# Half of each v load moved from the SP queue to GpSimd's own DMA queue

## The chip, the cores and the metric

The kernel runs on one core of a Trainium2 chip. The metric is the device time of one execution in microseconds (us), the median over the runs of a kernel. Lower is better.

## The reference

Two attentions in a row, then a mixture of experts with one expert per token. Cut to what is computed:

```python
# q, k, v: [8, 8, 576, 64], p: [8, 8, 32, 64], scale = 1/8
p_packed = softmax(scale * p @ k^T) @ v            # 32 packed rows per head
out      = softmax(scale * q @ p_packed^T) @ p_packed
x = out.transpose(0, 2, 1, 3).reshape(4608, 512)
logits = x @ w_gate + modality_bias[modality_id]    # 8 experts
e = argmax(logits); g = softmax(logits)[e]
y = g * (relu(x @ w1[e]) @ w2[e])                   # w1: 512 x 1024, w2: 1024 x 512
```

All inputs and the output are float32.

## The kernel before, in words

**Attention units.** A unit is one pair of batches (i = 0 to 3) and one group of four heads (g = 0, 1), so there are eight units, m = 0 to 7. A unit loads its k, q and v, each 1152 KB, each as two DMAs of 576 KB (u = 0, 1: the two batches of the pair). `load_tok` (L192 to L197) loads k and q: each of its two DMAs writes rows of 2304 bytes to all 128 partitions. `load_v` (L204 to L209) loads v: the DMA of u = 0 writes partitions 0 to 63, the one of u = 1 writes partitions 64 to 127. All of them are issued by SP (SyncE), whose DMAs go through one queue in order, as do the stores of the attention's result to scratch memory (`xout`, L379 and L380) and the loads of the experts' weights (`load_w`, L644).

**What a unit computes.** `trans` (L215) turns k and q on TensorE, `scores1` (L229, L239 to L246) makes the first softmax, `a1trans` (L260) turns it, and `pack` (L266 to L287, matmuls at L273) multiplies it with v. For each of nine column blocks, `pack` takes the half of u = 0 and the half of u = 1 in turn, so it wants both halves nearly from its first matmul. VectorE (DVE) then scales the result at L281 (tile `bd`), and `packT`, `gate`, `scores2`, `xpart` and `xout` (L289 to L383) make the second attention and store it. v's tile comes from a pool of even units or a pool of odd units with one buffer each, so the v load of unit m waits for `pack` of unit m - 2.

**Order.** The loop at L779 walks n from -6 to 11 and, for each n, a list of steps written by hand (`ORDER`, L401). A step's leading > or < says which unit it is for: `>>>>dk`, `>>>dq` and `>>dv` issue the loads of k, q and v for units n + 4, n + 3 and n + 2. So SP's order at the start is k0, packed rows p, k1, q0, v0, k2, q1, then the constants of `routing_consts` (L98: two stores of a padding list at L100, a bias load at L104, two loads of modality numbers at L108), then v1, k3, q2, v2 and so on. The program order of PE, DVE, ACT and SP is fixed by this list (`manual_schedule`, L778); that of GpSimd (POOL) is not among them, and a planner places its instructions. In the loop GpSimd has the casts and products of `routing_consts` (L119 to L128), which wait for the load at L108, and the scattered writes of `scatter` (L469, nine for each pair of batches). After the loop it fetches token rows (L660, L662).

**After the loop.** Units 0 to 6 go through the loop, the rest of unit 7 is woven into the first expert slots. From about 150 us on the expert matmuls (L695, L730) run one slot after the other.

Of the kernel before, what the change touches and what calls it, by code (L numbers as in the profile page):

```python
# [17 lines left out]
DRAM = bass.MemoryType.DRAM  # L18
ds = bass.ds
SYNC = mybir.DependencyInfo(mybir.DependencyClass.Sync, mybir.DependencyReason.DATA)  # L20


@with_exitstack
def packed_attn_moe_kernel(
# [14 lines left out]
    nc = tc.nc  # L39
# [9 lines left out]
    SP = S // NC  # L49
# [82 lines left out]
    NA = (NP // 2, NP - 1)  # L132
# [34 lines left out]
    def prep_p(ps1, n4):  # L167
# [5 lines left out]
        nc.vector.tensor_copy(out=pT[:, n4:n4 + 4, :], in_=t.rearrange("p (n c) -> p n c", n=4))  # L173
        yield

# [6 lines left out]
    def attention(i, g, lt, A, Z):  # L185
# [3 lines left out]
        hs = slice(HG * g, HG * g + HG)  # L189
        D_ = {}  # L190

        def load_tok(src, nm):  # L192
            t = A["ld"].tile([P, 2, 2, NC * D], F32, name="re" + nm)
            for u in range(2):
                nc.sync.dma_start(t[:, u], src[2 * i + u, hs].rearrange("h s d -> (h s d)").rearrange(
                    "(a r x) -> r a x", r=P, x=NC * D))
            return t  # L197

        def tile_of(nm, pool, shape, **a):
# [3 lines left out]

        def load_v():  # L204
            v_t = zp.tile([P, HG, NC * D], F32, name="ld_v")
            for u in range(2):
                nc.sync.dma_start(v_t[SP * u:SP * u + SP], v[2 * i + u, hs].rearrange("h s d -> h (s d)").rearrange(
                    "h (p x) -> p h x", x=NC * D))
            return v_t.rearrange("p h (c d) -> p h c d", c=NC)  # L209

        def trans(nm, f0, w):
# [173 lines left out]
        def load(nm):  # L385
            D_[nm + "r"] = load_v() if nm == "v" else load_tok(k if nm == "k" else q, nm)
            yield
# [23 lines left out]
    def ins_of(x):  # L411
        return getattr(x, "ins", x)
# [52 lines left out]
    def scatter(i):  # L465
        for c in range(NC):
            dsi = sm.tile([P, 1], I32, name=f"dsi{c}", bufs=2)
            nc.vector.tensor_copy(out=dsi, in_=dests[i][:, c:c + 1])  # L468
            ins = ins_of(nc.gpsimd.indirect_dma_start(  # L469
                out=lst, out_offset=bass.IndirectOffsetOnAxis(ap=dsi, axis=0),  # L470
                in_=meta[:, i * NC + c, :], in_offset=None))
            tc.declare_no_dep(ins, group="scat", reason="every row of the list is written once")
            tc.add_to_no_dep_group("scat", ins)
            if i >= NA[0]:
                tc.add_to_no_dep_group("late", ins)
            if i >= NA[1]:
                tc.add_to_no_dep_group("last", ins)
            scattered[i].append(ins)
            yield ins
# [178 lines left out]
    def fetch(tb, s, ph, mt, xt):  # L658
# [8 lines left out]
        if ph == 1:  # L667
            for z in scattered[NA[1] - 1]:
                tc.add_manual_dep(ins_of(ins[0]), z.name, SYNC, reason="rows of the list")

# [11 lines left out]
    def behind(ins, todo, n_each):  # L682
        for _ in range(n_each):
            z = next(todo, None)
            if z is not None:
                tc.add_manual_dep(z, ins.name, SYNC, reason="scatters with time between them")

# [54 lines left out]
    with ExitStack() as actx:  # L742
# [32 lines left out]
        for n in range(NA[0]):  # L775
            more[2 * n + 2] = route(n)
            spread[2 * n + 2] = scatter(n)
        with tc.manual_schedule(engines={ET.PE, ET.DVE, ET.Activation, ET.SP}):  # L778
            for n in range(-6, NU + 6):  # L779
                for z in ORDER.split():  # L780
                    nm = z.lstrip("<>")
# [33 lines left out]
    first = (0, SA[0], SA[1])  # L815
# [79 lines left out]
    with ExitStack() as actx:  # L895
# [4 lines left out]
        u = us[NU + 1]  # L900

        def table_b():
            for _ in routing(NA[1] - 1, lts[NA[1] - 1], ZL["ps1"]):
                pass
            T.append(table_phase("b", T[0]["last"], NA[1], T[0]["used"], SA[1] - SA[0]))
            todo.append(scatter(NA[1] - 1))
# [13 lines left out]
        with behind_both(first_x):  # L920
            split_w(W, 0, None, (1, 2, 3))
            for _ in routing(NA[1] - 1, lts[NA[1] - 1], ZL["ps1"]):
                pass
        todo.append(scatter(NA[1] - 1))
        for n in range(1, 4):
            ev = st_1(W, todo[0], 3, (2 * n,))
# [71 lines left out]
```

## Time and profile before

| what | us |
|---|---|
| median of 3 runs | 621.76 |
| lowest and highest run | 619.72, 625.98 |
| the profiled execution | 618.04 |
| its span, first to last instruction | 616.4 |
| around the span | 1.64 |
| TensorE busy in the span | 573.3 |
| VectorE busy | 252.3 |
| ScalarE busy | 219.9 |
| GpSimd busy | 148.1 |

PE is TensorE's matmuls and PEld its weight loads; DVE is VectorE, ACT ScalarE, POOL GpSimd, SP SyncE. An engine's busy time is an average over stages with different limits: in the attention stage the DMA engines are full, in the expert stage TensorE is. Times in the rows are counted from the start of the span. v0 is the v load of unit 0, and likewise k3 or q1; the first half of a v load is u = 0, the second u = 1.

### The profile page before, as it was taken

The numbers are of one execution on the slowest core, as the hardware profiler recorded it, in microseconds if no ns is written. First come the engines' busy times: TensorE is split into PE (matmuls) and PEld (weight loads), VectorE is DVE, ScalarE is ACT, GpSimd is POOL, SyncE is SP. The second block draws the span as 40 slices with busy tenths as digits, with TensorE's granted clock in tenths as the row PEclk, the third lists the DMA queues.
The fourth block names the chain that finished last, engine by engine and source line by source line (L and its number), as shares of the span: only waits on it lengthen the run. The fifth ranks groups of instructions, "written<-read, shape, count | busy, mean of one in ns | idle before, by whom it ended". The sixth has DMA issues, their size and how long they took to land. (4 is left out here: it accounts for less than half of the span.)

```text
span 616.4 us, 12544 instructions
## 1 busy us (share of the span) xinstructions
PE 573.3 (93%) x4820; PEld 499.8 (81%) x4820; DVE 252.3 (41%) x669; ACT 219.9 (36%) x401; POOL 148.1 (24%) x183
## 2 busy tenths in 40 slices
PE   4879898987999999999999999999999999999982
PEld 3657676665988989889889889989989989989981
DVE  1468998985965412145021173112112112112281
ACT  3648676755433111153121272122122112112360
POOL 2020041350552332232123122212211211311221
PEclk9979999976999999999999999999999999999997
DMA  9999999968766410028603027111201111111111
GB/s 292 248 262 314 313 347 308 299 144 299 250 225 174 155 53 20 36 85 341 275 25 99 36 74 287 64 43 37 66 38 36 51 39 52 48 40 53 41 49 56
DMA packets 49224, 87.47 MB, mean 142 GB/s; under 512 B 12528, under 2 KB 22320, under 8 KB 49136
## 3 DMA queue, kind: packets, MB, share of 16 engines
q1 hardware_dynamic: 39024, 63.92, 32.5%
q0 software_dynamic: 8528, 22.16, 11.3%
q8 instruction: 48, 0.79, 0.5%
q10 hardware_dynamic: 1584, 0.28, 0.2%
q14 instruction: 40, 0.33, 0.2%
HBM read 66.78 MB, written 19.56 MB: 140 GB/s over the span
## 5 line engine op out<-in xcount | busy, mean ns | idle before, releaser
L695 PE MATMUL ps_h<-x_hl,w1h 128*128 128x256 f32 x1088 | 199.6, 285 | 0.8 <-ACTq L892 0.7
L695 PEld LDWEIGHTS ps_h<-x_hl,w1h 128*128 128x128 f32 x1088 | 171.8, 193 | 4.5 <-ACT x_hl L677 1.0
L695 PE MATMUL ps_h<-x_hl,w1l 128*128 128x256 f32 x544 | 154.4, 284 | 0.0
L700 DVE SCALAR_TENSOR_TENSOR hl<-ps_h,hh 128x512 fp32r<-128x512 f32 x68 | 46.9, 690 | 245.8 <-ACT hh L699 245.7
L730 PE MATMUL ps_o<-w2h,hh 128*128 128x512 f32 x296 | 118.1, 399 | 3.0 <-ACT ot L734 2.2
L730 PE MATMUL ps_o<-w2h,hl 128*128 128x512 f32 x296 | 116.4, 393 | 0.0
L730 PE MATMUL ps_o<-w2l,hh 128*128 128x512 f32 x296 | 115.8, 391 | 0.3 <-DVEq L845 0.3
L695 PEld LDWEIGHTS ps_h<-x_hl,w1l 128*128 128x128 f32 x544 | 104.8, 193 | 0.0
L699 ACT ACTIVATE hh<-ps_h 128x512 fp32r<-128x512 f32 x68 | 40.6, 597 | 151.2 <-PE ps_h L695 149.7
L735 POOL DMA_INDIRECT out_dram<-ot,mt x37 | 40.7, 1100 | 183.6 <-ACT ot L734 119.1
L734 ACT ACTIVATE ot<-ps_o,mt 128x512 f32<-128x512 f32 x37 | 25.4, 688 | 149.6 <-PE ps_o L730 123.2
L730 PEld LDWEIGHTS ps_o<-w2h,hh 128*128 128x128 f32 x296 | 55.7, 188 | 14.7 <-ACT ot L734 3.5
L469 POOL DMA_INDIRECT lst<-meta,dsi x36 | 36.6, 1017 | 119.3 <-DVE dsi L468 63.2
L730 PEld LDWEIGHTS ps_o<-w2h,hl 128*128 128x128 f32 x296 | 55.6, 188 | 11.6
L730 PEld LDWEIGHTS ps_o<-w2l,hh 128*128 128x128 f32 x296 | 55.7, 188 | 10.9 <-DVEq L845 0.6
L662 POOL DMA_INDIRECT xt<-x_scr,mt x46 | 45.3, 984 | 74.1 <-DMA mt<-lst 28.2
L218 ACT COPY kT<-ps 128x512 f32<-128x512 f32 (+1 forms) x80 | 40.9, 555 | 24.5 <-PE ps L215 24.5
L678 DVE TENSOR_TENSOR x_hl<-ps_t,x_hl 128x512 fp32r<-128x512 f32 x42 | 27.5, 683 | 19.5 <-ACTq L845 12.0
L215 PE MATMUL ps<-ident,rek 128*128 128x128 f32 x144 | 23.2, 302 | 7.8 <-DMA rek<-in_k_dram 7.5
L660 POOL DMA_DIRECT2D mt<-lst x23 | 17.3, 753 | 54.0 <-DMA out_dram<-ot,mt 40.1
L354 PE MATMUL ps<-bd,a2T 64*128 64x136 f32 (+1 forms) x320 | 27.0, 320 | 3.1 <-DVE a2T L338 2.4
L273 PE MATMUL ps<-ld_v,a1T 64*64 64x128 f32 x576 | 21.8, 291 | 7.4 <-DMA ld_v<-in_v_dram 5.9
(187 smaller groups left out, 642.7 us busy)
## 6 DMA issues: line engine op xcount, KB each, us to landing
raw<-in_moe_w_dram SPq DMA_DIRECT2D x24, 1024.0 KB
rek<-in_k_dram SPq DMA_DIRECT2D x16, 576.0 KB
req<-in_q_dram SPq DMA_DIRECT2D x16, 576.0 KB
ld_v<-in_v_dram SPq DMA_DIRECT2D x16, 576.0 KB
x_scr<-xs SPq DMA_DIRECT2D x28, 256.0 KB
x_scr<-ld_v SPq DMA_DIRECT2D x4, 256.0 KB
x_scr<-xs SPq DMA_DIRECT2D x14, 64.0 KB
raw<-in_p_dram SPq DMA_DIRECT2D x2, 384.0 KB
```

What stands on the lines that cost most here:

```text
L215: nc.tensor.transpose(out=t[:, c * P:c * P + P], in_=src[:, (f0 + c) * P:(f0 + c) * P + P], identity=ident)
L218: nc.scalar.copy(out=T_[:, f0:f0 + w, :], in_=t[:, :w * P].rearrange("p (f r) -> p f r", f=w))
L354: nc.tensor.matmul(xp[rows, pr, z * XW:z * XW + XW], a2T[rs, t0:t0 + n], D_["bd"][rs, u, :], start=True, stop=True)
L469: ins = ins_of(nc.gpsimd.indirect_dma_start(out=lst, out_offset=bass.IndirectOffsetOnAxis(ap=dsi, axis=0), in_=meta[:, i * NC + c, :], in_ ...
L662: ins.append(nc.gpsimd.indirect_dma_start(out=xt[:, t], out_offset=None, in_=x_scr[0:NA[ph] * 2 * S] if ph < 2 else x_scr, in_offset=bass. ...
L678: iv = tt(out=M["xl"][:, :, ts], in0=ps, in1=M["xh"][:, :, ts].bitcast(F32), op=ALU.subtract)
L695: nc.tensor.matmul(ps[:, f], M[a][:, j, (f0 + f) * P:(f0 + f) * P + P], M[b][:, j], start=(n == 0), stop=(n == 3 * KD - 1))
L699: ia = nc.scalar.activation(out=M["hh"][:, fs], in_=ps, func=AF.Relu)
L700: iv = nc.vector.scalar_tensor_tensor(out=M["hl"][:, fs], in0=ps, scalar=0.0, in1=M["hh"][:, fs].bitcast(F32), op0=ALU.max, op1=ALU.subtract)
L730: nc.tensor.matmul(op, M[a][:, j, t * P:t * P + P], M[b][:, j, :], start=(n == 0), stop=(n == 3 * KF - 1))
L734: nc.scalar.activation(out=ot, in_=op, func=AF.Copy, scale=mt.bitcast(F32)[:, t, 2:3])
L735: nc.gpsimd.indirect_dma_start(out=out, out_offset=bass.IndirectOffsetOnAxis(ap=mt[:, t, 1:2], axis=0), in_=ot, in_offset=None, bounds_che ...
```

## The change

Of the two DMAs of a v load, the one of u = 1 (partitions 64 to 127) is now issued by GpSimd, on GpSimd's queue, and the one of u = 0 stays on SP. The GpSimd issues of v halves and the scattered writes of pairs 0 and 1 are chained in program order (`on_pool`), without a wait between them. For the two units of pair 0 (v0 and v1) the GpSimd issue also waits until the second half of that unit's q load has landed (`landed`). The chain does not name the casts of `routing_consts`.

```diff
+NOSYNC = mybir.DependencyInfo(mybir.DependencyClass.NoSync, mybir.DependencyReason.DATA)
...
+    landed = []
+    in_order = []
+
+    def on_pool(ins):
+        if in_order:
+            tc.add_manual_dep(ins, in_order[-1].name, NOSYNC, reason="the loop's order")
+        in_order.append(ins)
...
             for u in range(2):
-                nc.sync.dma_start(t[:, u], src[2 * i + u, hs].rearrange("h s d -> (h s d)").rearrange(
+                ins = nc.sync.dma_start(t[:, u], src[2 * i + u, hs].rearrange("h s d -> (h s d)").rearrange(
                     "(a r x) -> r a x", r=P, x=NC * D))
+            if nm == "q":
+                landed.append(ins_of(ins))
...
         def load_v():
             v_t = zp.tile([P, HG, NC * D], F32, name="ld_v")
-            for u in range(2):
-                nc.sync.dma_start(v_t[SP * u:SP * u + SP], v[2 * i + u, hs].rearrange("h s d -> h (s d)").rearrange(
+            for u, q_ in ((1, nc.gpsimd), (0, nc.sync)):
+                ins = q_.dma_start(v_t[SP * u:SP * u + SP], v[2 * i + u, hs].rearrange("h s d -> h (s d)").rearrange(
                     "h (p x) -> p h x", x=NC * D))
+                if u == 1:
+                    on_pool(ins_of(ins))
+                    if i == 0:
+                        tc.add_manual_dep(ins_of(ins), landed[g].name, SYNC, reason="k and q first")
...
+            if i < NA[0]:
+                on_pool(ins)
```

## Rows read from the trace of the kernel before

**Rows 1.** Windows by stage: length, busy us of each engine (instructions), PEclk, DMA share, GB/s.

```profile
36.00:44.00 8.00, 5.22 (x88) 4.12 (x88) 3.14 (x9) 1.76 (x4) 0.34 (x1) 0.59 1.05 331
...
60.00:128.00 68.00, 59.67 (x1002) 44.78 (x1002) 63.30 (x233) 46.78 (x100) 16.17 (x17) 0.96 1.04 310
...
152.00:582.00 430.00, 425.94 (x2799) 385.96 (x2799) 126.60 (x304) 110.90 (x183) 108.83 (x111) 1.00 0.29 98
```

**Rows 2.** Windows of the attention stage by which load is moving, same columns.

```profile
16.00:21.00 5.00, 4.84 (x47) 3.43 (x47) 1.32 (x5) 4.19 (x10) 0.00 (x0) 1.00 1.05 218
...
22.00:27.00 5.00, 4.83 (x99) 3.43 (x100) 2.49 (x6) 1.37 (x4) 0.00 (x0) 1.00 1.05 393
28.00:32.00 4.00, 4.00 (x64) 2.95 (x70) 2.58 (x6) 3.25 (x8) 0.18 (x2) 1.00 0.27 32
...
34.00:38.00 4.00, 1.43 (x10) 0.97 (x10) 3.93 (x9) 3.69 (x8) 2.27 (x3) 0.94 1.05 222
...
125.00:128.00 3.00, 2.36 (x50) 1.16 (x50) 2.90 (x12) 1.67 (x4) 0.86 (x2) 0.71 1.05 223
```

**Rows 3.** PE timeline, pack's matmuls of units 0, 1, 3 and 5.

```profile
22.17 0.88 PE L273 MATMUL ps<-ld_v,a1T 64*64 64x128 f32 x22 [1.21 <-DMA ld_v<-in_v_dram]
...
24.97 0.89 PE L273 MATMUL ps<-ld_v,a1T 64*64 64x128 f32 x24
...
36.51 0.40 PE L273 MATMUL ps<-ld_v,a1T 64*64 64x128 f32 x2 [1.48 <-DVE nb L242]
39.18 4.11 PE L273 MATMUL ps<-ld_v,a1T 64*64 64x128 f32 x70 [2.28 <-DMA ld_v<-in_v_dram]
...
68.91 2.20 PE L273 MATMUL ps<-ld_v,a1T 64*64 64x128 f32 x72
...
103.93 2.19 PE L273 MATMUL ps<-ld_v,a1T 64*64 64x128 f32 x70 [2.40 <-DMA ld_v<-in_v_dram]
```

**Rows 4.** Waits of DVE, 20 to 60 us: total us, times, longest.

```profile
DVE bd L281 <- PE ps L273: 5.5, 3, 4.8
```

**Rows 5.** Waits of DVE, 60 to 130 us, all of them.

```profile
DVE lt L367 <- ACT xs L365: 1.7, 4, 0.6
DVE r L252 <- ACT a L246: 1.0, 2, 0.8
DVE bd L281 <- PE ps L273: 0.5, 1, 0.5
```

**Rows 6.** SP timeline, DMA issues around the first v loads.

```profile
11.70 1.37 SPq L207 DMA_DIRECT2D ld_v<-in_v_dram  x2
...
15.45 10.05 SPq L100 DMA_DIRECT2D lst<-pad  x2
25.54 3.56 SPq L104 DMA_DIRECT2D bias<-n_moe_modality_bias_dram  x1
29.15 1.50 SPq L108 DMA_DIRECT2D mid<-in_moe_modality_id_dram  x2
30.69 1.29 SPq L207 DMA_DIRECT2D ld_v<-in_v_dram  x2
```

**Rows 7.** POOL timeline: the casts' first and last, a plain DMA and the gather behind it.

```profile
31.82 0.35 POOL L119 CAST m<-mid 64x16 f32<-64x16 int32 x2 [27.04 <-DMA mid<-in_moe_modality_id_dram]
...
35.55 0.79 POOL L128 TENSOR_TENSOR bias_all<-bias_all,bias_t 128x288 f32<-128x288 f32 x1
...
132.25 0.78 POOL L660 DMA_DIRECT2D mt<-lst  x1 [2.01 <-DMA lst<-meta,dsi]
...
134.62 1.03 POOL L662 DMA_INDIRECT xt<-x_scr,mt  x1 [0.67 <-DMA mt<-lst]
```

**Rows 8.** Windows around two falls of TensorE's clock, columns as in rows 1.

```profile
33.00:37.00 4.00, 1.67 (x12) 1.04 (x10) 3.93 (x9) 3.93 (x8) 3.17 (x7) 1.00 1.00 242
...
39.00:44.00 5.00, 4.82 (x86) 3.94 (x86) 0.61 (x2) 0.00 (x0) 0.00 (x0) 0.50 1.05 392
...
71.00:75.00 4.00, 2.03 (x29) 0.95 (x25) 3.90 (x11) 1.50 (x5) 0.00 (x0) 1.00 1.08 384
75.00:78.00 3.00, 2.91 (x14) 2.91 (x15) 2.72 (x19) 1.50 (x6) 0.00 (x0) 0.51 1.03 257
```

**Rows 9.** DVE timeline: one small operation beside a busy POOL, and alone.

```profile
34.99 0.52 DVE L328 TENSOR_SCALAR dn<-dn 128x18 f32<-128x18 f32 x1
...
45.30 0.17 DVE L328 TENSOR_SCALAR dn<-dn 128x18 f32<-128x18 f32 x1
```

## The prediction

> **What bounds the kernel now.** I read the windows by stage first. From 152 to 582 us TensorE is busy 425.9 of 430 us at full clock, with the DMA engines 29% busy [rows 1]: the expert stage is bound by TensorE and loads no v, so the change can only move its start. In the attention stage, from 60 to 128 us, the DMA engines stand at 1.04 and VectorE (DVE) at 63.3 of 68 us [rows 1]. Two resources look full there, so the waits must say which ends last. DVE waits 3.2 us in all from 60 to 130 us, and only 0.5 of it leads back to pack, the user of v [rows 5]; from 20 to 60 us pack holds it 5.5 us, 4.8 of them in one piece [rows 4]. That piece is the second unit's pack: from 36 to 44 us DVE is busy 3.1 of 8 us [rows 1]. So after 60 us DVE sets the pace and a faster load is mostly absorbed, and around 38 us a load sets it.
>
> Next, the windows by kind of load. While k and q (128 partitions) are loaded the queue moves 393 GB/s; while v is loaded it moves 218, 222 and 223, at an equal DMA share [rows 2], the first, second and last of eight such stretches. A v half is 576 KB = 0.590 MB, so it takes 0.590/217 = 2.72 us and a unit's v 5.4 us, where k takes 3.0. From 28 to 32 us the DMA engines are nearly idle, 0.27 and 32 GB/s [rows 2]: SP had issued v0 from 11.70 us, and is then held for 10.05, 3.56 and 1.50 us by the constants' small DMAs before it issues v1 at 30.69 [rows 6].
>
> Last, the PE timeline: pack waits for v three times, 1.21 us at 22.17 (unit 0), 2.28 us at 39.18 (unit 1) and 2.40 us at 103.93 (unit 5) [rows 3]. Sum 5.9 us. That is all that v costs TensorE directly.
>
> **The change part by part.**
>
> *v1, the main term.* Two matmuls of pack 1 run at 36.51, with the first half, and the other 70 wait until 39.18 [rows 3]: what is late is the second half, behind the first on SP's queue, behind the constants. With the change GpSimd issues it once q1 has landed. The rate falls from 393 GB/s to nothing by 28 us [rows 2], so q1 has landed by about 28.0. For GpSimd's path the nearest row is a plain DMA of 4 KB: begun at 132.25, and the gather that needs it starts at 134.62, so 2.37 us or less from begin to landing [rows 7]. The half then lands at about 28.0 + 2.4 + 2.7 = 33.1 us, largely in the idle stretch, where it takes nothing from anyone. The first half still lands before 36.5, as it does now. So pack 1 runs through from 36.5 and the wait goes: **-2.28 us**. Ends: 0 (the half comes no sooner) and -4.7 (the clock, next). DVE idles 4.8 us there [rows 4], so it can take even the larger gain, and after it no load must wait for the compute: v2's second half may also go out in the idle stretch, as pack 0, whose tile it reuses, ends at 24.97 + 0.89 = 25.9 us [rows 3]. That frees 2 x 2.72 = 5.4 us of SP's queue for k and q, more than the 2.3 us by which the compute moves up.
>
> *The clock at pack 1.* [...] Pack 1's 70 matmuls take 4.11 us there, 72 take 2.20 at full clock [rows 3]. If the clock stayed up, another 4.11 - 2.14 = 2.0 us would go, and some 0.5 on the scores behind. I don't take it: the idle before 36.5 stays, since its last part is a wait for DVE (1.48 us, [rows 3]), and at 71 to 75 us 2.03 busy us in 4 were followed by 0.51 as well [rows 8]. It is a case of its own.
>
> *v0.* q0 has landed near 16 us, where the rate falls to 218 with v0 [rows 2]. GpSimd's half then flows from about 16.0 + 2.0 = 18 us, when the first half is nearly through (16.0 + 2.7 = 18.7), and shares the engines with k2. Now both halves need 16.0 + 5.4 = 21.4 us, and pack's wait ends at 22.17 [rows 3]. With half of 393 GB/s GpSimd's half needs 0.590/196 = 3.0 us, to 21.0; with half of the time at 217 GB/s 5.4 us, to 23.4, which is 2.0 later than 21.4. Taken: 0, nearer to the first. Ends: -1.2 (the whole wait) and +2.0.
>
> *v2 to v7.* Packs 2, 3, 4, 6 and 7 don't wait for v (unit 3's at 68.91 stands for the five in [rows 3]), so a v that comes sooner is worth nothing there by itself. At 103.93 TensorE waits 2.40 us, but DVE works on through it: its whole wait for pack after 60 us is 0.5 us [rows 5]. Taken: -0.5, ends -1.2 and 0.
>
> *What is added.* Eight issues leave SP (1.37 us for a pair, [rows 6]) and eight come to GpSimd, at 0.78 [rows 7] to perhaps 1.5 us each, as the half has as many rows to describe as 256, but longer ones. GpSimd is busy 16.2 of 68 us from 60 to 128 [rows 1], which covers 8 x 1.5 = 12; without that cover the scattered writes would be late, but the list is read only after 130 us. What is queued behind a waiting v half on GpSimd: for v1 the casts of the constants, which wait for their load until 31.82 anyway [rows 7]; for v4 to v7 scattered writes, each held at most until pack of two units earlier, which is long done. A busy GpSimd slows a small DVE operation from 0.17 to 0.52 us [rows 9]; eight issues, one or two such meetings: **+0.3**, ends 0 and 8 x 0.35 = 2.8.
>
> *Whether two queues help each other.* No row shows two half loads at once. The nearest are 218 and 393 GB/s [rows 2], so side by side the halves take between 2.7 and 5.4 us. My sum takes little from this: v1 gains because GpSimd is not held by SP's constants, not because the halves overlap.
>
> [...]
>
> *Sum.* -2.28 + 0 - 0.5 + 0.3 = -2.5 us. The profiled execution of 618.04 (616.4 of span and 1.64 around it) becomes 615.5. It lies 3.7 us below the median of the runs shown, 621.76, and from that the forecast is 621.76 - 2.5 = **619.3 us**. The three runs lie 619.72 to 625.98, 1% apart, so 1% (6.2 us) is about what can be told from no change.
>
> **The rivals.**
>
> *B, the clock stays up.* A pack 1 that runs on at 36.5 keeps TensorE above its low level, and v0 comes 0.8 us sooner. [...] -2.5 - 2.0 - 0.5 - 0.8 = -5.8, so 616.0.
>
> *C, the halves take turns.* Packets of both queues go through the same engines, and a half load beside other traffic gets half the time at 217 GB/s. Then v0 is 2.0 us late (23.4 against 21.4), the compute up to pack 1 moves by as much, and of the 2.28 us 0.3 is left, which DVE's slowing of 0.3 takes: 0.0, so 621.8. For it: the DMA share is already 1.05 at 218 GB/s [rows 2]. [...]
>
> *D, slower: v1's half stands behind the casts on GpSimd.* The chain names v halves and scattered writes, not the casts, and the planner places those. Behind them the half is issued at 35.55 + 0.79 = 36.3 [rows 7], lands at 36.3 + 2.4 + 2.7 = 41.4, or 44.1 beside k3, so pack 1 is 2.2 to 4.9 us later than 39.18, at a point where DVE has nothing else to do [rows 4]. It decides once the issue is later than 39.18 - 5.1 = 34.1 us. +3.5, so 625.3. Against it: q1 lands some 4 us before the casts can start, and a planner that places what is ready first puts the half ahead.
>
> *E, it doesn't do what it says.* GpSimd's half is early, but the first half, still behind SP's constants, comes after 36.5 and pack 1 waits for that one. Two matmuls with it ran at 36.51 [rows 3], so at best a fraction is lost. I count it with C.
>
> **How the numbers follow.** My forecast 0.48, B 0.20, C with E 0.20, D 0.12. The forecast's own range is 616 to 622. To hold 8 in 10 it must reach past B and C, take v0's ends (-1.2, +2.0) and 2.8 us of DVE's slowing, and much of D: 612 to 625. Faster by over 1% needs 615.5 or less: half of B and a tenth of the forecast, with the spread of the runs, 0.22. Slower by over 1% needs 628: half of D, and C with the slowing on top, 0.10. Within 1% is the rest, 0.68.
>
> **What would show it right or wrong.** Right: one large DVE wait for pack before 60 us shrinks from 4.8 to about 2.5; DMA traffic appears between 28 and 33 us; pack 1's matmuls start near 36.5 without a wait for v, still at 0.50; waits of DVE after 60 us stay near 3 us. B: PEclk is 1.00 from 37 to 44. C: unit 0's pack starts after 23 us, and half loads beside each other stay near 217 GB/s. D: GpSimd's issue of v1 stands after L128. The forecast is wrong at its root if DVE's waits after 60 us fall or grow by several us, for then the loads, not DVE, set the pace of the loop; or if the expert stage itself, 430 us that I leave untouched, changes its length.

## The result and the profile after

| what | before, us | after, us |
|---|---|---|
| median (11 runs each) | 621.17 | 625.56 |
| lowest and highest run | 619.64, 625.98 | 623.75, 628.76 |
| the profiled execution | 618.04 | 625.72 |
| its span | 616.4 | 624.0 |
| start of the first expert matmul | 150.90 | 155.50 |
| from there to the end of the span | 465.5 | 468.5 |

The ratio is 1.0064, interval 1.0041 to 1.0088: 4.0 us slower (2.5 to 5.5). That is less than 1%, but the median lies 0.6 us above the range of 612 to 625, and on the other side of before than the forecast of 619.3. The profiled execution of before lies 3.1 us under its median and that of after 0.2 above, so the two profiles differ by 7.6 us of span where the medians differ by 4.4: what follows reads places and shares from the profiles and sizes from the ratios. Of the 7.6 us, 4.6 arise before the expert stage and 3.0 in it.

The PE timeline of after (start and duration in us; in brackets the idle time before and what ended it), matmuls of pack, line 291 now: three rows of unit 0, one each of units 1, 3 and 5, and three of the seven pieces of unit 7:

```profile
27.02 1.55 PE L291 MATMUL ps<-ld_v,a1T 64*64 64x128 f32 x22 [5.95 <-DMA ld_v<-in_v_dram]
...
29.54 1.56 PE L291 MATMUL ps<-ld_v,a1T 64*64 64x128 f32 x24
...
31.85 0.89 PE L291 MATMUL ps<-ld_v,a1T 64*64 64x128 f32 x24
...
41.83 2.20 PE L291 MATMUL ps<-ld_v,a1T 64*64 64x128 f32 x72
...
70.99 2.20 PE L291 MATMUL ps<-ld_v,a1T 64*64 64x128 f32 x72
...
105.20 2.19 PE L291 MATMUL ps<-ld_v,a1T 64*64 64x128 f32 x72
...
137.41 1.75 PE L291 MATMUL ps<-ld_v,a1T 64*64 64x128 f32 x52
...
140.34 0.45 PE L291 MATMUL ps<-ld_v,a1T 64*64 64x128 f32 x3 [0.57 <-issue]
...
143.99 0.58 PE L291 MATMUL ps<-ld_v,a1T 64*64 64x128 f32 x5 [1.02 <-issue]
```

Against [rows 3]: pack 0 waits 5.95 us, not 1.21, and goes on at 27.02, not 22.17. Its first two blocks take 1.55 and 1.56 us where 0.88 stood, so pack 0 ends at 32.74 instead of 25.86, 6.9 us late: 4.85 for the load and 2.0 for the clock. By pack 1 4.2 us are won back, as it runs without its wait of 2.28 and at full clock (2.20 us at 1.00): it is 2.65 us behind (41.83), and pack 5, without its wait of 2.40, is 1.3 behind (105.20). Unit 7's pack runs in seven pieces with standstills marked "issue", 7.2 us in all for 2.2 us of work.

Windows of after, columns as in [rows 1]:

```profile
22.00:27.00 5.00, 0.00 (x0) 0.00 (x0) 0.00 (x0) 0.00 (x0) 0.00 (x0) 0.77 1.01 284
28.00:32.00 4.00, 4.00 (x46) 2.84 (x43) 0.79 (x3) 1.31 (x3) 1.03 (x4) 0.56 0.49 91
34.00:38.00 4.00, 4.00 (x58) 3.16 (x58) 2.59 (x7) 3.35 (x9) 2.68 (x7) 1.00 1.02 225
...
36.00:44.00 8.00, 7.25 (x145) 5.25 (x145) 7.70 (x15) 6.40 (x15) 2.65 (x4) 1.00 1.06 324
60.00:128.00 68.00, 58.32 (x981) 43.87 (x965) 61.89 (x228) 46.01 (x99) 17.19 (x18) 1.00 0.99 303
152.00:582.00 430.00, 422.50 (x2789) 380.79 (x2789) 127.34 (x304) 112.45 (x183) 108.44 (x109) 1.00 0.30 102
```

From 22 to 27 us no engine does anything but wait, while the queues move 284 GB/s; before, k2 flowed there at 393 [rows 2]. The clock falls in that standstill (0.77 as a mean, then 0.56). From 36 to 44 us DVE is busy 7.7 us, not 3.1: the late compute catches up with the loads there. From 60 to 128 us nothing got faster: 303 GB/s at 0.99 against 310 at 1.04.

The waits of DVE in after, 20 to 60 us:

```profile
DVE pT L174 <- PE ps L171: 13.1, 3, 8.0
...
DVE bd L299 <- PE ps L291: 1.0, 2, 0.8
```

In before, 20 to 60 us, the first of these read:

```profile
DVE pT L173 <- PE ps L170: 6.3, 3, 3.5
```

The waits of DVE in after, 60 to 130 us:

```profile
DVE bd L299 <- PE ps L247: 1.8, 1, 1.8
DVE lt L385 <- ACT xs L383: 1.7, 4, 0.6
DVE bd L299 <- PE ps L291: 0.8, 1, 0.8
```

The prediction named one sign of success: the large DVE wait for pack of 4.8 us [rows 4] would shrink to about 2.5. It shrank to 0.8, and the kernel became slower. The wait had moved: PE works in a fixed order, the turns of p stand behind the first matmuls of pack 0, and DVE now waits 8.0 us in one piece for those (3.5 before), under another line. In sum DVE waits 16.9 us from 20 to 60 us, not 14.6, and 5.6 us from 60 to 130, not 3.2. A wait that shrinks is a gain only if the sum over the engine shrinks with it.

The POOL timeline of after, issues of the halves of v0 and v1, and the first cast:

```profile
17.16 0.84 POOL L221 DMA_DIRECT2D ld_v<-in_v_dram  x1 [12.37 <-DMA req<-in_q_dram]
29.36 0.65 POOL L221 DMA_DIRECT2D ld_v<-in_v_dram  x1 [11.37 <-DMA req<-in_q_dram]
31.62 0.35 POOL L120 CAST m<-mid 64x16 f32<-64x16 int32 x2 [1.61 <-DMA mid<-in_moe_modality_id_dram]
```

v1's half stands ahead of the casts, so rival D did not happen. v0's half is issued at 17.16 us. The DMA view of after by queue (q1 is SP's, q0 GpSimd's; packets, MB, share of the 16 engines' time), for 17 to 21 us:

```profile
q1 hardware_dynamic: 564, 1.23, 104.0%
```

and for 21 to 22 us:

```profile
q1 hardware_dynamic: 136, 0.28, 75.9%
q0 software_dynamic: 29, 0.13, 40.1%
```

For four microseconds after the issue not one packet of GpSimd's queue moves, and SP's queue, which holds v0's first half, k2 and q1 by then, has the engines to itself. By the start of each packet of the large size in the trace, v0's half begins 4.4 us after its issue (21.58) and ends at 26.08. The same reading for the eight halves: where SP's queue held no large load (v1, v7) 1.4 us from issue to first packet, beside a queue with large loads in it 3.4 to 5.8 us.

In the expert stage after has four PE waits that before has not (waits of PE from 155.5 us on; before's list from 150.9 us holds only the other five):

```profile
PE ps L458 <- DVE gs L476: 1.1, 1, 1.1
...
PE ps_t L695 <- DMA xt<-x_scr,mt: 0.7, 1, 0.7
PE ps_h L715 <- issue: 0.4, 1, 0.4
PE ps_h L715 <- DVE x_hl L698: 0.3, 1, 0.3
```

Together 2.5 of the 3.0 us by which the stage grew. The three with a named waiter belong to what is woven in behind unit 7: its routing and the first gathers. They are not the change's own, though: in the profiles of two kernels below that are not slower, the one with v1 alone and the first with the constants behind v1, such waits stand too, with 2.0 and 1.5 us, and the stage is 466.2 and 466.3 us long.

### The profile page after: what moved, and what is told of

Same layout as the page of the kernel before. It is cut to its first block, busy times and chain, and to the rows that moved or that the text cites. A ratio compares the mean times of both kernels' runs of the same rounds, so it can differ in the third digit from the quotient of the medians.

```text
span 624.0 us, 12563 instructions
## 1 busy us (share of the span) xinstructions
PE 570.7 (91%) x4820; PEld 496.5 (80%) x4820; DVE 251.9 (40%) x669; ACT 219.2 (35%) x401; POOL 153.6 (25%) x191
## 5 line engine op out<-in xcount | busy, mean ns | idle before, releaser
L698 DVE TENSOR_TENSOR x_hl<-ps_t,x_hl 128x512 fp32r<-128x512 f32 x42 | 27.5, 684 | 18.7 <-ACTq L865 12.0
L291 PE MATMUL ps<-ld_v,a1T 64*64 64x128 f32 x576 | 23.7, 287 | 10.1 <-DMA ld_v<-in_v_dram 6.0
L372 PE MATMUL ps<-bd,a2T 64*128 64x136 f32 (+1 forms) x320 | 25.6, 311 | 4.8 <-DVE key L535 1.3
```

The source lines that it names most:

```text
L291: nc.tensor.matmul(pp[cols, u, :P].rearrange("p (h d) -> p h d", h=2), a1T[rows, blk(c), cols], v_t[rows, 2 * pr:2 * pr + 2, c, :], start= ...
L372: nc.tensor.matmul(xp[rows, pr, z * XW:z * XW + XW], a2T[rs, t0:t0 + n], D_["bd"][rs, u, :], start=True, stop=True)
L698: iv = tt(out=M["xl"][:, :, ts], in0=ps, in1=M["xh"][:, :, ts].bitcast(F32), op=ALU.subtract)
```

## The experiments

Each kernel was compared with the kernel before on the same chip. The chips differ (medians of before 616.2 to 621.2), so ratios are compared, not times.

**One part of the change at a time.** Four kernels change only for which units the half goes to GpSimd: all but unit 0, unit 1 alone, unit 0 alone, and from unit 2 on.

```diff
-            for u, q_ in ((1, nc.gpsimd), (0, nc.sync)):
+            both = ((1, nc.gpsimd), (0, nc.sync)) if 2 * i + g in (1,) else ((0, nc.sync), (1, nc.sync))
+            for u, q_ in both:
...
-                if u == 1:
+                if q_ is nc.gpsimd:
```

All but unit 0:

> As the changed kernel, but both halves of v0 stay on SP; the halves of v1 to v7 still go through GpSimd. Late v0 (the half of v0 is behind SP's backlog on the engines, 4.4 us from issue to its first packet, and holds pack 0 for 6.0 us): the wait of pack 0 for v falls back to about 1.2 us, the gain at pack 1 (2.3 us) stays, and the time is 618 to 620 us, below the kernel before. Later halves (a half beside k or q slows both to about 230 GB/s, and the PE stands still inside packs 2, 4, 6, 7): pack 0 is mended, but the time stays at 623 to 625 us. Tail order (the planner placed the expert matmuls and the routing of the tail otherwise): the tail is planned as in the kernel before here, so the 3 us that the changed kernel loses after 155 us are gone too.

Unit 1 alone:

> Only the second half of v1 goes through GpSimd, all other v halves through SP. Late v0: the same as the run with v0 alone on SP, 618 to 620 us, since the later halves cost nothing. Later halves: 618 to 620 us here and clearly more there. Both: pack 1 starts near 36.5 us without a wait for v, and the half lands between 28 and 34 us, in the stretch where SP's constants leave the DMA engines idle. If even this gains nothing (621 us), the 2.3 us wait of pack 1 was not on the path.

Unit 0 alone:

> Only the second half of v0 goes through GpSimd. Late v0: 625 to 628 us, slower than the changed kernel or equal to it, with a wait of pack 0 near 6 us and the clock at 0.50 behind it. Later halves: no more than 622 us, as six of the eight halves are back on SP. The tail is planned as in the changed kernel.

From unit 2 on:

> Only the second halves of v2 to v7 go through GpSimd; v0 and v1 load as in the kernel before. Late v0: 620 to 622 us, no change against the kernel before. Later halves: 624 to 626 us. The tail is planned as in the kernel before. In either case the half loads should start 3 to 6 us after their issue where SP's queue is full.

| halves on GpSimd | ratio | interval | us of 621.2 |
|---|---|---|---|
| v0 | 1.0038 | 1.0015 to 1.0061 | +2.4 |
| v1 | 0.9998 | 0.9978 to 1.0019 | -0.1 |
| v2 to v7 | 1.0037 | 1.0013 to 1.0061 | +2.3 |
| v1 to v7 | 1.0073 | 1.0047 to 1.0099 | +4.5 |
| all (the change) | 1.0064 | 1.0041 to 1.0088 | +4.0 |

In us of 621.2 the four kernels come to 625.7, 621.1, 623.6 and 623.5. The first is near what the theory of the later halves expected, the other three lie outside both: neither v0 nor the later halves carry the loss alone.

v0 alone gives the standstill of the changed kernel again, in its PE timeline:

```profile
27.39 1.55 PE L292 MATMUL ps<-ld_v,a1T 64*64 64x128 f32 x22 [5.38 <-DMA ld_v<-in_v_dram]
```

But the loss of v0 is not the whole: without it the kernel is as slow. In that run, with v1 to v7, pack 0 waits 2.29 us and pack 1 is the late one:

```profile
42.50 4.12 PE L292 MATMUL ps<-ld_v,a1T 64*64 64x128 f32 x72 [4.89 <-DMA ld_v<-in_v_dram]
```

It stands 3.3 us behind before's 39.18, at the low clock (4.12 us for the pack; before's 4.11 [rows 3] stood at 0.50 [rows 8]), and packs 2 and 3 keep the 3 us. With v1 alone it is milder:

```profile
39.47 4.12 PE L292 MATMUL ps<-ld_v,a1T 64*64 64x128 f32 x72 [3.95 <-DMA ld_v<-in_v_dram]
```

There the half on GpSimd does land early, from 31.9 to 35.3 us by its packets. Which half pack 1 waited for is in the DMA view of that run, 32 to 33 us:

```profile
q0 software_dynamic: 23, 0.11, 50.2%
q1 hardware_dynamic: 7, 0.00, 0.4%
```

SP's queue is at the constants and passes 7 packets in a microsecond in which GpSimd's passes 23 (0.11 MB). A microsecond earlier it passed 579, of some 70 bytes each (0.04 MB). v1's first half stands behind these small packets and starts at 34.7 us, when the other half is all but through, so it ends at 39 us where the second half used to. The pair was turned round, not made faster. As the wait was not taken away, this run does not tell whether it lay on the path.

**Is it the loop's order or the chip?** Both kernels once more, side by side on one chip.

> The kernel before, profiled a second time. Run to run (the profiled execution of 618.04 lay 3 us under its own median, and its packs had no gap): one profile differs from the next by 2 to 4 us, packs 4 and 6 show gaps without a waiter here too, and the first expert matmul comes between 151 and 154 us. Later halves (those gaps come from the halves on GpSimd): no gap inside any pack, first expert matmul at 151 us.

> The changed kernel, profiled a second time. If the gaps of pack 7 (some 5 us between 139 and 144 us) belong to the change, they come again, and the first expert matmul is at 155 to 156 us; if they are chance, pack 7 takes 2.2 us and the first expert matmul is at 151 to 152 us. Pack 0 waits 5.5 to 6.5 us for v in either case.

Spans 614.2 and 622.3: pack 0 waits 1.54 and 6.44 us, the first expert matmul starts at 149.11 and 154.89, and the expert stage is 465.1 and 467.4 long. The places of the loss repeat. The pieces in unit 7's pack do not: it runs in one stretch in this execution of the changed kernel. Nor does the gain at pack 5: there it waits 2.53 us for v again.

**The constants off SP's queue.** All of the kernel before, with the five small DMAs of `routing_consts` issued by GpSimd and v whole on SP.

```diff
-            nc.sync.dma_start(lst.rearrange("(e r) w -> r e w", e=E)[z:z + P], pad)
+            nc.gpsimd.dma_start(lst.rearrange("(e r) w -> r e w", e=E)[z:z + P], pad)
...
-        nc.sync.dma_start(bias2, mod_bias[None].broadcast_to([P, 2, E]))
+        nc.gpsimd.dma_start(bias2, mod_bias[None].broadcast_to([P, 2, E]))
```

(and likewise the two loads of modality numbers.)

> The kernel before, all v halves on SP, but the small DMAs of the constants (padding, bias, modality numbers) go through GpSimd's queue. Constants hold v1: SP issues v1 near 16 us instead of 30.69, the idle stretch of the DMA engines between 28 and 33 us is gone, pack 1 starts without a wait for v, and the time falls by 2 to 5 us, to 616 to 619 us. Rival (packets of the two queues take turns, so the small ones slow the large): the stretch to pack 0 gets longer by as much and nothing is gained, 621 us.

1.0020, interval 0.9999 to 1.0041: no gain, as the rival had it. SP issues v1 at 18.1 us instead of 30.7, and pack 1 waits 0.7 us only, at full clock (2.19 us for 70 matmuls), but pack 0 comes 3 us later than in the repetition of before (25.85 against 22.88). By their packets GpSimd's small DMAs move from 7 to 14 us, beside k and p, and the first turn of p waits 2.30 us for its load and comes at 13.18 us (10.82 in before).

**The constants behind v1.** If v1's first half is held up by the small packets ahead of it, it must flow once they are behind it. The first of two kernels does this to the kernel before, the second to the one with v1 alone on GpSimd.

```diff
                 yield
+            for _ in range(3):
+                yield
             routing_consts(pzp)
```

> The kernel before, all v halves on SP, with one step moved: the constants' small DMAs (padding list, bias, modality numbers) are issued behind v1 and ahead of k3, not ahead of v1. Theory 1 (pack 1 waits because v1 stands behind the constants, and the DMA engines have free time from 28 to 32 us): v1 is issued near 16 us, flows right behind q1 from 28 to 33.5 us, pack 1 starts near 36.5 us without a wait for v, as the prediction wanted it from the change; 2 to 3 us less than the kernel before, ratio 0.995 to 0.997. Rival (the free time only moves: SP stays held by the constants until v1 has drained, so k3 comes as much later as v1 comes sooner): pack 1 has no wait, but DVE waits for k3's unit before 75 us instead, ratio 0.999 to 1.001.

> As the run before it, with the second half of v1 issued by GpSimd as in the run with v1 alone. So no small packets stand ahead of v1's first half on SP's queue. Theory 1 (in the run with v1 alone the first half was late because the constants' packets ahead of it got one turn against each large packet of GpSimd's half): the first half now flows from 28 us beside the second, both end near 33.5 to 34.5 us, pack 1 runs from about 36.5 us without a wait for v, and the time is within 0.2% of the run before it. Rival (SP's half is held back by GpSimd's whatever stands ahead): the first half starts only when the second has ended, pack 1 waits 2 us or more, 1.5 to 3 us slower than the run before it. A rival of the sign: if GpSimd's queue is of any use here, it is faster than the run before it by 1 us or more.

The first, in its PE timeline (packs 1 and 2) and then its SP timeline (k3's issue):

```profile
37.47 2.20 PE L273 MATMUL ps<-ld_v,a1T 64*64 64x128 f32 x72
56.20 2.30 PE L273 MATMUL ps<-ld_v,a1T 64*64 64x128 f32 x72
```

```profile
36.93 1.08 SPq L195 DMA_DIRECT2D rek<-in_k_dram  x2
```

Pack 1's wait is gone and its clock is full (2.20 us; 1.00 from 36 to 40 us), just what the prediction's main term and rival B wanted. Yet pack 2 starts at 56.20, 1.1 us later than before's 55.13: k3 is issued at 36.93, not 32.08, because SP is held by the constants behind v1. So the rival's mechanism is there: the idle stretch moves and remains (14 and 8 GB/s in the two microseconds from 35 us on). The ratio of 0.9984 (0.9959 to 1.0009) lies between what the two expected and tells neither from no change.

The second, packs 1 and 2:

```profile
37.52 2.32 PE L292 MATMUL ps<-ld_v,a1T 64*64 64x128 f32 x72
51.91 2.02 PE L292 MATMUL ps<-ld_v,a1T 64*64 64x128 f32 x53
```

No wait for v at pack 1 against 3.95 us: the only difference to the run with v1 alone is the place of the constants, so it was they that held the first half up. How is not shown: SP issues the first half at 15.54 us here and at 31.14 there, behind GpSimd's at 30.30. One part of the expectation failed: the halves do not flow side by side. The first has flowed by 31 us, the second is issued at 31.98 and ends at 36.45. So the recorded rival, that SP's half waits for GpSimd's whatever stands ahead of it, is not tested here. Here pack 2 gains 3.2 us. The time was 0.9988 of before's, 0.9958 to 1.0017, so it was run again, beside a kernel with the constants two loads further back.

```diff
-            for _ in range(3):
+            for _ in range(4):
                 yield
...
+                        if m == 2 and nm == "dq":
+                            next(more[-1], None)
```

> The same kernel as in the earlier run with v1's half on GpSimd and the constants behind v1's first half, to tell a gain from the spread between executions. Theory 1 (pack 1 without a wait, at full clock, is worth the 2.3 us of the prediction once nothing holds the first half up): ratio to before 0.995 to 0.998, upper end below 1. Rival (its good profile was chance, k3 behind the constants eats the gain): 0.998 to 1.001, profile 614 us or more.

> As the other of this pair, with the constants' small DMAs two loads later, behind k3 and q2 on SP's queue (the sum that needs them, bias_all, is read at 68.5 us in the trace of before). Theory 1: v1 as there, pack 1 near 36.5 to 37.5 us without a wait, and k3 flows right behind v1 by 37 us, so pack 2 starts by 52 us and nothing before 75 us waits for a load; ratio 0.993 to 0.997, at least as fast as the other. Rival (the constants' 10 us on SP now stand before v2 and k4, the free time only moves on): pack 2 in time, but pack 3 or 4 is then as late as before, within 0.2% of the other.

The repetition gave 1.0014, 0.9983 to 1.0044: no gain. Pack 1 is early again, but unit 7's pack runs in pieces this time, three of its PE rows:

```profile
36.79 2.19 PE L292 MATMUL ps<-ld_v,a1T 64*64 64x128 f32 x70 [1.02 <-DMA ld_v<-in_v_dram]
...
133.61 1.75 PE L292 MATMUL ps<-ld_v,a1T 64*64 64x128 f32 x52
...
138.97 1.12 PE L292 MATMUL ps<-ld_v,a1T 64*64 64x128 f32 x4 [0.89 <-issue]
```

With the constants behind q2 it is slower, 1.0038 (1.0013 to 1.0064). Both theories missed: SP issues k3 by 20.96 us but q2 only at 31.99, as its tile is still in use, and the constants behind it; v1's half, issued by GpSimd at 32.46 beside k3 and q2, sends its first packet only at 36.7, and pack 1 waits 3.55 us and starts at 42.21. It is the lead of v0's half once more, at another place.

**Without the wait for q.** The changed kernel, with the issue of v0's and v1's halves not held back.

```diff
-                    if i == 0:
-                        tc.add_manual_dep(ins_of(ins), landed[g].name, SYNC, reason="k and q first")
```

> The changed kernel without the wait for the landing of q in v0 and v1 (all eight second halves still on GpSimd). Both go out as soon as GpSimd comes to them, some 5 us from the start. Theory 1 (the loss of the changed kernel is the lead of 3.4 to 5.8 us behind q's landing, and v1's first half behind the constants' packets): v0's second half lands before 16 us and v1's with it, k0, p, k1 and q0 are later by their 2 x 2.7 us in part, pack 0 runs at 23 to 26 us without a wait for v, v1's first half is alone behind the constants and lands by 36, pack 1 starts by 38; 3 to 5 us faster than the changed kernel, 619.5 to 622.5 against 621.2 of before. Rival (the halves of v2 to v7 alone carry the loss): pack 0 and pack 1 come in time and the time stays within 1 us of the changed kernel's.

1.0097, interval 1.0063 to 1.0131: no faster than the changed kernel, though for neither theory's reason. Both halves are issued from 3.2 us on and land by 15.5, and pack 0 needs no wait for v, but it is later still. In the PE timeline, the first turn of p (10.82 us before) and pack 0:

```profile
17.05 1.09 PE L171 MATMUL ps<-ident,raw 128*128 128x128 f32 x4 [5.96 <-DMA raw<-in_p_dram]
...
28.73 0.89 PE L290 MATMUL ps<-ld_v,a1T 64*64 64x128 f32 x24
```

The 1.18 MB go ahead of p and q0, which are needed first. Early too, the halves took their time from the loads beside them: the first turn of p came 6.2 us later.

**The queues by themselves.** A kernel of loads only, with the maxima over them; it leaves out the whole computation.

> Only loads, no computation of the reference: seven stages with a barrier between them. Stage 1, eight halves on SP: 217 GB/s. Stage 2, the same with every second half on GpSimd: 217 to 260 GB/s if halves in two queues take turns, 380 if they fill each other's gaps. Stage 3, the second queue is ACT's: the same question without GpSimd. Stages 4 and 5, eight full loads on SP with two halves on GpSimd or ACT: the first packet of the half comes 4 us or more behind its issue if it waits for what SP's queue has handed to the engines, 1.4 us if not; the rate while both run falls from 390 to about 230. Stages 6 and 7, stores of 64-byte rows with and without halves on GpSimd: some 500 packets per us without, 50 to 100 with them.

Its windows: both halves on SP (8 to 26 us), one on SP and one on GpSimd (46 to 62), full loads on SP alone (120 to 122), and the same beside halves of GpSimd (126 to 134):

```profile
8.00:26.00 18.00, 15.85 (x9) 0.00 (x0) 1.00 1.04 225
46.00:62.00 16.00, 13.86 (x8) 1.39 (x3) 1.00 1.04 228
...
120.00:122.00 2.00, 1.57 (x2) 0.00 (x0) 1.00 1.01 387
126.00:134.00 8.00, 6.71 (x4) 0.62 (x1) 1.00 1.03 279
```

Two queues move 228 GB/s of halves where one moves 225, and by their large packets they do so in turns. SP's half of the second pair is issued at 45.27 us and begins at 48.92, when GpSimd's half before it (46.30 to 49.03) is all but through; GpSimd's, issued at 45.54, follows at 51.55. The 279 GB/s are no shared rate either but a mean over turns: GpSimd's half until 127.2 us, two full loads of SP from 127.1 to 131.1, GpSimd's next half from 130.6 to 133.4. That half was issued at 128.09 and so began 2.5 us later, neither the 1.4 nor the 4 us expected, as SP's loads ended. And SP's next loads, issued at 130.23 and 130.65, wait for it until 132.9, where a full load on SP alone began 1.0 us after its issue. The DMA view of 131 to 132 us:

```profile
q0 software_dynamic: 49, 0.23, 104.8%
q1 hardware_dynamic: 4, 0.00, 0.8%
```

No small packets stand in SP's queue there. So SP's loads can stand still beside GpSimd's half without any, and that the small packets were the reason in the run with v1 alone is not shown. With ACT as the second issuer the sum is no higher (208 from 84 to 103 us), so it does not hang on GpSimd. The part on small packets gave nothing: the padding stores ran at the start, not beside the halves.

## Why the prediction was wrong

Three terms of the sum failed, by like amounts: v0 by 2.4 us, v1 by 2.2, v2 to v7 with DVE's +0.3 by 2.5. The first is the one whose way from the step to its price the traces show best.

**v0: "Taken: 0, nearer to the first. Ends: -1.2 and +2.0."** This is the step that failed. The half was to flow from "about 16.0 + 2.0 = 18 us". For the 2.0 us of GpSimd's lead it names no row; its nearest one, 2.37 us or less for a 4 KB load [rows 7], was taken beside an empty SP queue. The wait for the landing ended at 17.16 and the first packet moved at 21.6: the lead was 4.4 us beside SP's full queue, and 1.4 (v1, v7) where that queue held no large load. The half itself took 4.5 us, between the 3.0 and 5.4 foreseen. The price was +4.85 us at pack 0, outside the ends, and the clock took 2.0 more there; +2.4 us in the time when it is done alone. It was costed as a load that shares from the start, and it is a load that starts last.

**v1: "The first half still lands before 36.5, as it does now."** Also wrong: rival E, which I counted with C at 0.20, is what happened in the run with v1 alone. The second half did come in the idle stretch as predicted, ending at 35.3 us, not 33.1, but the first half, behind the constants on SP, stood still beside it, and the gain of 2.28 measured 0.1. That these 2.28 us, and the clock of rival B, were there to be had in the profile is shown by the two kernels with the constants behind v1; that they reach the end of the program is not: neither was faster beyond its interval.

**"That frees 2 x 2.72 = 5.4 us of SP's queue."** Wrong: nothing is freed. In the load-only kernel two queues moved 228 GB/s of halves where SP's alone moved 225, both at a DMA share of 1.04, and the halves took turns. Rival C had this mechanism right and its price too small: it counted half the rate from 18 us on, not the silence before it.

**v2 to v7: "Taken: -0.5", with +0.3 for DVE's slowing.** Measured +2.3 (0.8 to 3.8). In the run from unit 2 on packs 2 to 7 start within 2 us of before's, so the price is not a late load inside the loop. In its one profile the first expert matmul comes 16.8 us after the start of unit 7's pack, not 14.8, and the expert stage is 467.6 us, not 465.5. But that does not show the cause: the profile of the kernel with the constants on GpSimd, which has no half there, has a stage of 468.4 us, and v1 alone, no slower than before, has the same four further PE waits as this run (2.0 us against 2.1). The prediction had "the expert stage itself" as a way to be wrong, and DVE's waits after 60 us, which were to stay near 3 us: they are 5.2 us in this run, but 5.5 us with v1 alone too. What v2 to v7 pay for stays open.

**What held.** The reading of before held: loads set the pace around 38 us, the expert stage is bound by TensorE (422.5 busy us of 430 in after), DVE is full from 60 us on (61.9 of 68), and rival D's order on GpSimd did not occur. Whether the order that the chain fixes on GpSimd costs something by itself, no run shows. The wait of pack 1 went as foreseen in the changed kernel, but there because the compute was late, not because v was early; pack 5's went in one profile and was back, 2.53 us, in the other.

**What stays open.** First, the effects do not add: v1 and v2 to v7 alone sum to +2.2 us, together they cost +4.5. In the run with both, v2's half follows v1's on GpSimd's queue at once (31 to 39 us by their packets) and v1's first half waits for the two, which fits, but no run separates v2. Second, the standstills marked "issue". They cut up unit 7's pack in four of the ten profiles with a half on GpSimd, and in none of the four without; in those four the first expert matmul comes 18.1 to 18.7 us after that pack's start, else 12.7 to 16.8. They recur in one execution of a kernel and not in the next, as the two of the changed kernel show. Shorter ones cut other packs: between 20 and 156 us PE stands still with no waiter for 0.5 to 4.6 us in ten of the eleven profiles with DMAs moved to GpSimd (the constants alone too: 1.6 us), and not at all in the three without. So they go with GpSimd's DMAs and may be part of the price, but with v1 alone they take 2.2 us and the time is unchanged. Their cause was not found. Third, the order of DVE and PE behind the loop, which a planner makes, is another one than before's in the three kernels with v0's half on GpSimd (the change, v0 alone, and the one without the wait for q); the kernel with v1 to v7 has before's order on DVE and is as slow. What the order adds was not isolated; whatever it is lies within the +2.4 us of v0.

## What to carry to other kernels

Here a second DMA queue added a place in the queue, not bandwidth (228 GB/s of halves on two queues, 225 on one): ask which loads the new one takes its time from, and take its lead from a row in which the other queue is as full as it will be. Loads that are wanted as a pair are as late as the later one, and sending one of them early by another queue can leave the other as late as the pair was: with v1 alone one half ended at 35.3 us and the other at 39. When a wait shrinks, look for its time under the other names of the same engine before calling it won.

## What was not expected of the hardware

An issue on GpSimd's queue moved its first packet 1.4 us after it began where SP's queue held no large load, and 3.4 to 5.8 us after beside one that did. It is no matter of GpSimd alone: in the load-only kernel SP's half, too, began 3.65 us after its issue, when GpSimd's was all but through. Once both flowed, they shared packet for packet in the changed kernel from 22 to 23 us:

```profile
q0 software_dynamic: 34, 0.16, 65.0%
q1 hardware_dynamic: 33, 0.07, 29.7%
```

while in the load-only kernel one of them stood all but still from 131 to 132 us (49 packets against 4). What decides between the two, and why GpSimd's queue was silent for four microseconds from 17 to 21 us in the changed kernel, no run shows.
